# A transformer block on one core: heads normalised with VectorE's block transposes, and moved to the contraction's rows by small transfers

## The chip, the cores and the metric

The kernel runs on one core of a Trainium2 chip. The metric is the device time of one execution in microseconds (us). Five engines work beside each other, each through its own instructions in order: TensorE (PE in the profile, its weight loads PEld), VectorE (DVE), ScalarE (ACT), GpSimd (POOL) and SyncE (SP), which issues nearly all transfers (DMA). Matrix products land in PSUM, where the program has tiles of 512 fp32 a row: two times two of tag s, two of f, one each of m and a. Everything else lies in SBUF.

## The reference

Pre-norm attention with 32 query heads of width 18 over one shared key and value head, then a gated feed-forward without a nonlinearity. S = 2048, D = 576, F = 4608, all in fp32:

```python
def _A_ref(x, wq, wk, wv, wo):
    q = (x @ wq).reshape(B, S, H, Dh).transpose(0, 2, 1, 3)
    k = x @ wk
    v = x @ wv
    scores = jnp.einsum("bhqd,bkd->bhqk", q, k) * (Dh ** -0.5)
    p = _softmax(scores, axis=-1)
    o = jnp.einsum("bhqk,bkd->bhqd", p, v)
    return o.transpose(0, 2, 1, 3).reshape(B, S, H * Dh) @ wo
...
def _B_ref(x, w_gate, w_up, w_down):
    h = (x @ w_gate) * (x @ w_up)
    return h @ w_down
...
h = x + _A_ref(_layernorm(x), A_wq, A_wk, A_wv, A_wo)
h2 = h + _B_ref(_layernorm(h), B_w_gate, B_w_up, B_w_down)
```

## The kernel before

**Tiling.** The 2048 rows are worked in four blocks of 512 (b = 0 to 3), the 32 heads in eight groups of four (g = 0 to 7). For precision most products are made of a high and a low part of each operand (split, L91 and L92: a cast to the high part, a subtraction for the low part).

**Attention.** For one group and 128 keys, two steps of `pair` compute the scores of two heads each (L506, into PSUM of tag s, two buffers) and their exponential on ACT (L507). `flush` multiplies with the values (L511): four heads stand below each other in acc, 32 rows a head, of which row 0 is the softmax's sum (V has a column of ones) and rows 1 to 18 are the head. After 16 key tiles acc (128 x 512: rows are 4 heads x 32, columns are queries) is copied to os by VectorE (L522).

**Normalising a group** (`normal_heads`). Four PE transposes bring os to pt, with queries on the rows (L549); VectorE takes the reciprocal of the sums (L556; in block 0 a maximum with 1e-30 first, L553 and L554), and four multiplications write the heads to ob, 72 columns a group (L558). Two groups fill a chunk of 128 of the 576 columns. `chunk` transposes it back on PE (to, L140, four transposes), and splits it to o_hl (to oT in block 0), where the 576 columns are on the rows that the output projection contracts over. Chunk 4 has the last 64 columns twice, since its high and low part share a tile.

**Projecting.** `project` multiplies a chunk with its part of wo (yo, L625) and adds to the residual h on VectorE (L626). The weights wo of a chunk are loaded (wor, L587) when the chunk is split, and split one round later (wos).

**Order.** The program's order is written out by hand, and each engine follows it. Block 0's attention runs beside the query projections; the attention of block b + 1 runs inside the feed-forward of block b (`ffn`): 36 steps f, each with 54 products for gate and up (L818), a `pair` every four of them, and, in every second step, a down projection (`down`, L778) whose adds alternate between VectorE (L781) and ACT with GpSimd (L785, L786). Two steps of this kind are a period of some 31 us. What a group leaves to be done stands in a list, aux, and `run_aux` takes one entry at a time, of those whose round has come: at the end of each step f, and from step 26 (WITHIN) on also in the middle of a step (j = 12), there without the projections. Down weights (wdo, L709), gate and up weights (wr, L695) and the queries of the next group (q, L430 and L436) are loaded by SP, in the program's order.

**PSUM.** pt and to take the single buffer of tag m, or, at the end of a step (`at_end`), one half of a buffer of tag s (`ps_x`).

**The end.** In the last block, the last down pair (L744) has products for four row tiles s and two column halves n; ys of the last row tiles are halves of a tile of tag s, and each is added to h (L768) before the next product starts.

Of the kernel before, what the change touches and what calls it, by code (L numbers as in the profile page):

```python
# [16 lines left out]
F32 = mybir.dt.float32  # L17
# [3 lines left out]
ALU = mybir.AluOpType  # L21
# [13 lines left out]
HD = D // 2  # L35
# [22 lines left out]
class Block:  # L58
# [19 lines left out]
    def ps_y(self, i, name):  # L78
        return self.ps_m(name) if i % 3 == 1 else self.ps_f(name)

    def ps_x(self, name):

        return self.ps_s(name)[:, 0] if self.at_end else self.ps_m(name)

    def ps_a(self, name):
        return self.ps.tile([P, TB], F32, tag="a", bufs=1, name=name)

# [44 lines left out]
    def ln_apply(self, src, dst, mean, rstd):  # L132

        self.dve.tensor_scalar(dst[:, 0:D], src, mean, rstd, ALU.subtract, ALU.mult)
        self.dve.tensor_copy(dst[:, D:], dst[:, 512:D])

    def transposed(self, src, to, c, psum):

        for s in range(NQ):
            self.pe.transpose(psum[:, s * P:(s + 1) * P], src[:, s, c * P:(c + 1) * P], self.ident)  # L140
        if c < 4:
            self.split(*to, psum)
        else:
            self.split_tail(*to, psum)


    def keys_values(self):
# [257 lines left out]
    def again(self, g):  # L405

        q = self.pp.tile([P, 2, TB], F32R, tag="P", name=f"qa{g}")
        self.load_q(q, 0, g)
        self.load_m(q, 0, g)
        acc = self.ps_a(f"acca{g}")  # L410
        for t in range(NT):
            Ps = []
            for pr in range(2):
                s_ = self.ps_s(f"sa{g}_{t}_{pr}")
                p_ = self.pp.tile([P, 2, TB], F32, tag="P", name=f"Pa{g}_{t}_{pr}")
                self.scores(s_, p_, q, t, pr)
                Ps.append(p_)
            self.values(acc, Ps, t)
            del Ps, p_, s_
        os_ = self.os.get(g)  # L420
        if os_ is None:
            os_ = self.pp.tile([P, TB], F32, tag="P", name=f"osa{g}")
        self.dve.tensor_copy(os_, acc)
        if g not in self.os:
            self.normal_heads(0, g, os_)

# [87 lines left out]
    def flush(self, n):  # L514

        for b, g, t, Ps in self.pend[:n]:
            if t == 0:
                self.acc = self.ps_a(f"acc{b}_{g}")
            self.values(self.acc, Ps, t)
            if t == NT - 1:  # L520
                os_ = self.os[g] = self.op.tile([P, TB], F32, tag="os", bufs=1, name=f"os{b}_{g}")
                self.dve.tensor_copy(os_, self.acc)  # L522
                self.aux.append((self.round + 1, lambda b=b, g=g, o=os_: self.normalise(b, g, o), None))
        del self.pend[:n]

# [9 lines left out]

    def normalise(self, b, g, os_):
        if g == 0:
            self.ob = self.op.tile([P, NQ, 640], F32, tag="ob", name=f"ob{b}")
        self.normal_heads(b, g, os_)
        del self.os[g]  # L540
        for c in (g // 2,) * (g % 2) + (4,) * (b == 0 and g == NG - 1):
            self.aux.append((self.round, lambda c=c: self.chunk(b, c), None))

    def normal_heads(self, b, g, os_):

        pe, dve, ob = self.pe, self.dve, self.ob
        pt = self.ps_x(f"pt{b}_{g}")
        for s in range(NQ):
            pe.transpose(pt[:, s * P:(s + 1) * P], os_[:, s * P:(s + 1) * P], self.ident)  # L549
        p4 = pt.rearrange("p (s j c) -> p s j c", s=NQ, j=4)  # L550
        rc = self.op.tile([P, NQ, 4], F32, tag="rc", bufs=2, name=f"rc{b}_{g}")
        if b == 0:
            dve.tensor_scalar(rc, p4[:, :, :, 0], 1e-30, None, ALU.max)  # L553
            dve.reciprocal(rc, rc)  # L554
        else:
            dve.reciprocal(rc, p4[:, :, :, 0])  # L556
        for s in range(NQ):
            dve.tensor_tensor(ob[:, s, 72 * g:72 * g + 72].rearrange("p (j c) -> p j c", c=DH),  # L558
                              p4[:, s, :, 1:1 + DH],
                              rc[:, s, :].unsqueeze(2).broadcast_to([P, 4, DH]), ALU.mult)  # L560
        if g == NG - 1:
            dve.tensor_copy(ob[:, :, D:], ob[:, :, 512:D])

    def chunk(self, b, c):

# [13 lines left out]
        return [self.o_hl[:, 0], self.o_hl[:, 1]] if c < 4 else [self.o_hl[:, 0]]  # L579

    def chunk_of(self, b, c):
        self.transposed(self.ob, self.heads_to(b, c), c, self.ps_f(f"to{b}_{c}") if b == 0 and c == 4 else self.ps_x(f"to{b}_{c}"))


    def load_wo(self, c):
# [146 lines left out]
    def down(self, b, pair):  # L732

        pe, dve, act, sp, pool = self.pe, self.dve, self.act, self.sp, self.nc.gpsimd
        h = self.h[b]
        W = [self.wdo.pop((b, pair, j), None) for j in range(7)]
        if pair == NC - 1:
            ys = {}

            def part(s, n, i):  # L740

                ms = [(self.A[:, k, 2 * i + s // 2], W[(1, 0, 2, 3)[2 * i + n]][:, l]) for k, l in ((0, 0), (0, 1), (1, 0))]
                for j, (m, k) in enumerate(ms):
                    pe.matmul(ys[s, n][:, :HD], m[:, s % 2 * P:(s % 2 + 1) * P], k, start=(i == j == 0), stop=(i == 1 and j == 2))  # L744

            if b == NB - 1:
                e = self.ps_s("ye")
                for k, y in enumerate((e[:, 0], e[:, 1], self.ps_f("ye2"), self.ps_f("ye3"), self.ps_m("ye4"), self.ps_a("ye5"))):
                    ys[k // 2, k % 2] = y
                    part(k // 2, k % 2, 0)  # L750
            for s in range(NQ):
                for n in range(2):
                    if (s, n) not in ys:
                        if b < NB - 1:
                            ys[s, n] = self.ps_y(2 * s + n, f"y{b}_{pair}_{s}_{n}")
                        else:
                            e = self.ps_s("ye6") if n == 0 else e
                            ys[s, n] = e[:, n]
                        part(s, n, 0)
                    part(s, n, 1)  # L760
                    hs, y = h[:, s, n * HD:(n + 1) * HD], ys.pop((s, n))[:, :HD]
                    if b < NB - 1 and n:
                        z = self.tmp[:, self.n_tmp % 5]
                        self.n_tmp += 1
                        act.copy(z, y)
                        pool.tensor_tensor(hs, hs, z, ALU.add)
                    else:
                        dve.tensor_tensor(hs, hs, y, ALU.add)  # L768
                    yield
                sp.dma_start(self.out[b * TB + s * P: b * TB + (s + 1) * P, :], h[:, s, :])  # L770
            return
# [26 lines left out]
    def ffn(self, b):  # L798
        pe, act, dve = self.pe, self.act, self.dve
        X, hid, todo = self.X, [], None  # L800
        for f in range(NF):
# [11 lines left out]
            for c in range(9):  # L813
                for wk, xk in ((0, 0), (0, 1), (1, 0)):
# [7 lines left out]
                        self.split_w(n_ + 1)  # L822
                    if j == 5 and k:
                        self.left_first(n_ - 1, hid[0])
                    if j == 12 and f >= WITHIN:
                        self.run_aux(within=True)
                    if j == 21 and b == f == 0:
                        self.flush(len(self.pend))
# [18 lines left out]
                drain(self.down(b, *todo))  # L847
                self.load_wd(self.n_wd + 7)
            if f < NF - 1:
                self.at_end = True  # L850
                self.run_aux()
                self.at_end = False
            todo = (f // 2,) if k else None
        if b + 1 < NB:
            both(self.spread(b + 1), self.down(b, *todo))
# [92 lines left out]
    def run(self):  # L948
# [8 lines left out]
        self.h, self.qt, self.normed, self.wr, self.ws, self.wdo, self.wo_r, self.wos = {}, {}, {}, {}, {}, {}, {}, {}  # L957
        self.n_pair, self.half, self.pend, self.aux, self.round = 0, [], [], [], 0
        self.tqs = []
        self.at_end = False  # L960
        self.p2, self.p_next, self.wo_from, self.due = None, -1, 10 ** 6, 0.0
        with ExitStack() as st:
            pool = lambda name, bufs, **k: st.enter_context(tc.tile_pool(name=name, bufs=bufs, **k))
# [83 lines left out]

ORDER = (0, 3, 4, 2, 5, 6, 1)
WD_BUFS = 10
WITHIN = 26  # L1050
# [109 lines left out]
```

## Time and profile before

| | |
|---|---|
| median of 3 runs | 2378.72 us (2378.16 to 2379.43) |
| the profiled execution | 2379.29 us |
| its span in the trace | 2377.5 us |
| granted TensorE clock, mean | 0.994 |
| PE busy | 2319.2 us, 98% |
| ACT busy | 1434.3 us, 60% |
| VectorE busy | 1150.8 us, 48% |
| GpSimd busy | 644.5 us, 27% |
| SP queue (hardware DMA) | 326.6 MB, 42.6% of 16 engines |

Times in the trace's rows are us from the span's start; a row of the timeline has start, length, engine, line, operation, tiles written and read, shapes, count, and in brackets the idle time of its engine before it with what ended that. A row of a group has the tiles, the shape, the count, busy time and mean length (ns), and idle time. SPq is SP's queue of issues. Names are the program's own, without buffer numbers.

### The profile page before, as it was taken

The numbers are of one execution on the slowest core, as the hardware profiler recorded it, in microseconds if no ns is written. First come the engines' busy times: TensorE is split into PE (matmuls) and PEld (weight loads), VectorE is DVE, ScalarE is ACT, GpSimd is POOL, SyncE is SP. The second block draws the span as 40 slices with busy tenths as digits, with TensorE's granted clock in tenths as the row PEclk, the third lists the DMA queues.
The fourth block names the chain that finished last, engine by engine and source line by source line (L and its number), as shares of the span: only waits on it lengthen the run. The fifth ranks groups of instructions, "written<-read, shape, count | busy, mean of one in ns | idle before, by whom it ended". The sixth has DMA issues, their size and how long they took to land.

```text
span 2377.5 us, 46287 instructions
## 1 busy us (share of the span) xinstructions
PE 2319.2 (98%) x18425; PEld 1630.6 (69%) x18425; DVE 1150.8 (48%) x2130; ACT 1434.3 (60%) x1869; POOL 644.5 (27%) x803
## 2 busy tenths in 40 slices
PE   5999989999999999999999999999999999999999
PEld 4333434677777777777776777767777788888888
DVE  7545534344443444544444445433444367565565
ACT  4787867766667665676666666566666622232322
POOL 3535400122212222222222122212222233343333
PEclk9999999999999999999999999999999999999999
DMA  4677860433333333533333333453333344655553
GB/s 139 207 256 249 282 214 19 139 123 107 114 99 117 118 123 113 170 123 118 119 105 116 103 123 118 135 157 118 122 114 110 95 156 161 200 191 184 174 166 125
DMA packets 154086, 340.23 MB, mean 143 GB/s; under 512 B 14760, under 2 KB 47016, under 8 KB 153864
## 3 DMA queue, kind: packets, MB, share of 16 engines
q1 hardware_dynamic: 151272, 326.59, 42.6%
q0 software_dynamic: 2592, 10.62, 1.6%
q8 instruction: 147, 2.41, 0.4%
q14 instruction: 75, 0.61, 0.1%
HBM read 272.63 MB, written 55.67 MB: 138 GB/s over the span
## 4 chain that ended last, share of the span: by engine, by line
PE 82%; DVE 1%; ACT 1%; DMA 1%; issue 0%; SPq 0%; ACTq 0%; DVEq 0%
PE y L778 17%; PE pg L818 16%; PE acc L511 15%; PE gu L818 12%; PE s L506 9%; PE pu L818 9%; PE yo L625 3%; PE y L744 1%; PE pt L549 1%; ACT P L507 1%; PE tx L674 0%; PE to L140 0%; PE ye L744 0%; DMA X<-X 0%; DMA out_dram<-h 0%
## 5 line engine op out<-in xcount | busy, mean ns | idle before, releaser
L507 ACT ACTIVATE P<-s 128x1024 f32<-128x1024 f32 x1024 | 1027.3, 1026 | 337.3 <-PE s L506 259.4
L818 PE MATMUL pu<-X,ws 64*128 64x512 f32 x2565 | 701.3, 391 | 0.0
L818 PE MATMUL pg<-X,ws 64*128 64x512 f32 x2565 | 701.3, 391 | 0.0
L786 POOL TENSOR_TENSOR h<-h,tmp 128x288 f32<-128x288 f32 x408 | 318.5, 811 | 938.3 <-ACT tmp L785 937.0
L818 PEld LDWEIGHTS pg<-X,ws 64*128 64x128 f32 x2565 | 475.8, 186 | 57.3 <-issue 1.5
L511 PE MATMUL acc<-P,V 128*32 128x512 f32 x4096 | 492.4, 600 | 4.8 <-DVE os L522 4.0
L818 PEld LDWEIGHTS pu<-X,ws 64*128 64x128 f32 x2565 | 473.7, 186 | 30.2
L506 PE MATMUL s<-q,kT 56*128 56x512 f32 x2048 | 442.1, 425 | 10.0 <-SPq L396 6.4
L778 PEld LDWEIGHTS y<-wdo,room 128*128 128x128 f32 x2856 | 386.0, 188 | 48.7 <-issue 45.8
L778 PE MATMUL y<-wdo,room 128*128 128x288 f32 x2856 | 403.4, 300 | 1.3 <-DVE h L781 1.2
L785 ACT COPY tmp<-y 128x288 f32<-128x288 f32 x408 | 162.7, 399 | 326.6 <-PE y L778 321.4
L781 DVE TENSOR_TENSOR h<-h,y 128x288 f32<-128x288 f32 x544 | 235.3, 454 | 243.6 <-PE y L778 241.1
L506 PEld LDWEIGHTS s<-q,kT 56*128 56x128 f32 x2048 | 196.9, 185 | 204.8 <-ACT P L507 109.8
L818 PE MATMUL gu<-X,ws 64*128 64x512 f32 x2646 | 308.8, 389 | 2.0 <-DVE hf L840 1.7
L818 PEld LDWEIGHTS gu<-X,ws 64*128 64x128 f32 x2646 | 256.0, 184 | 47.9 <-issue 4.1
L511 PEld LDWEIGHTS acc<-P,V 128*32 128x32 f32 x4096 | 114.6, 109 | 253.1 <-issue 232.0
L91 POOL CAST ws<-wr 128x1152 fp32r<-128x1152 f32 x144 | 165.7, 1151 | 436.8 <-PE pu L818 177.4
L840 DVE TENSOR_TENSOR hf<-pu,g 128x512 f32<-128x512 f32 x95 | 65.7, 692 | 380.1 <-ACT g L836 376.8
L92 DVE TENSOR_TENSOR ws<-wr,ws 128x1152 fp32r<-128x1152 f32 x144 | 194.9, 1354 | 60.4 <-POOL ws L91 60.4
L92 DVE TENSOR_TENSOR room<-S,room 128x1024 fp32r<-128x1024 f32 x68 | 83.3, 1225 | 143.7 <-ACT room L91 143.7
L836 ACT COPY g<-gu 128x512 f32<-128x512 f32 x49 | 28.9, 590 | 133.5 <-PE gu L818 133.5
L91 ACT CAST room<-hf 128x256 fp32r<-128x256 f32 (+1 forms) x144 | 73.9, 513 | 45.0 <-DVE hf L840 44.7
(169 smaller groups left out, 1594.3 us busy)
## 6 DMA issues: line engine op xcount, KB each, us to landing
wdo<-wd_dram SPq DMA_DIRECT2D x492, 288.0 KB
wr<-in_wgu_dram SPq DMA_DIRECT2D x144, 576.0 KB
wd_dram<-wd_room SPq DMA_DIRECT2D x20, 1008.0 KB
q<-q_dram SPq DMA_DIRECT2D x64, 216.0 KB
q_dram<-qs SPq DMA_DIRECT2D x16, 504.0 KB
X<-X SPq DMA_DIRECT2D x28, 256.0 KB
wd_dram<-wd_hi SPq DMA_DIRECT2D x7, 1008.0 KB
wd_dram<-wd_src SPq DMA_DIRECT2D x7, 1008.0 KB
```

The costliest lines, as they stand in the source:

```text
L91: (copy or self.cast)(hi, src)
L92: self.dve.tensor_tensor(lo, src, f32(hi), ALU.subtract)
L506: self.pe.matmul(s_[:, i], self.kT[o:o + 56, t * P:(t + 1) * P], q[o:o + 56, pr], start=True, stop=True)
L507: self.act.activation(p_, s_, AF.Exp, scale=SCALE)
L511: self.pe.matmul(acc[32 * j:32 * j + 32, :], self.V[:, t, :], Ps[j // 2][:, j % 2, :], start=(t == 0), stop=(t == NT - 1), skip_group_chec ...
L625: pe.matmul(y[:, :HD], m, k, start=(i == 0), stop=(i == len(ms) - 1))
L778: pe.matmul(y[:, :HD], m[:, t * P:(t + 1) * P], k, start=(first and j == 0), stop=(j == 2), skip_group_check=True)
L781: dve.tensor_tensor(hs, hs, y[:, :HD], ALU.add)
L785: act.copy(z, y[:, :HD])
L786: pool.tensor_tensor(hs, hs, z, ALU.add)
L818: pe.matmul(ps, w[o:o + 64, wk, c], X[o:o + 64, xk, c], start=(j == 0), stop=(j == 26))
L840: dve.tensor_tensor(hf, pu, g, ALU.mult)
```

## The change

os is made by a transpose of VectorE in blocks of 32 x 32 straight from acc, in place of the copy. Then each row of os is a query modulo 32, and its 512 columns are 16 pieces of 32, a piece for each run of 32 queries, with the sum in column 0 and the head in columns 1 to 18. One reciprocal and one multiplication normalise all of it in place, and a second block transpose brings the heads back below each other, into a free part of ob. From there 18 rows of 512 at a time are moved by SP to the rows that the contraction wants: a head is one transfer, or two where it crosses a chunk's end, and twice as many in chunk 4; 40 a block. A chunk is then split from ob as it stands. No PE transpose is left in either step. With them go `ps_x`, `at_end` and `transposed`. `run_aux` is called in the middle of every step f, and in block 0 a chunk is due two rounds later. In the last pair of the last block both halves are multiplied before either is added.

```diff
@@ flush, again
-                self.dve.tensor_copy(os_, self.acc)
+                self.dve.transpose(os_, self.acc)
@@ normalise
-            self.ob = self.op.tile([P, NQ, 640], F32, tag="ob", name=f"ob{b}")
+            self.ob = self.op.tile([P, 5, TB], F32, tag="ob", name=f"ob{b}")
...
-            self.aux.append((self.round, lambda c=c: self.chunk(b, c), None))
+            self.aux.append((self.round + (2 if b == 0 else 0), lambda c=c: self.chunk(b, c), None))
@@ normal_heads
-        pt = self.ps_x(f"pt{b}_{g}")
-        for s in range(NQ):
-            pe.transpose(pt[:, s * P:(s + 1) * P], os_[:, s * P:(s + 1) * P], self.ident)
-        p4 = pt.rearrange("p (s j c) -> p s j c", s=NQ, j=4)
-        rc = self.op.tile([P, NQ, 4], F32, tag="rc", bufs=2, name=f"rc{b}_{g}")
+        o = os_.rearrange("p (k c) -> p k c", c=32)
+        rc = self.op.tile([P, TB // 32], F32, tag="rc", bufs=2, name=f"rc{b}_{g}")
         if b == 0:
-            dve.tensor_scalar(rc, p4[:, :, :, 0], 1e-30, None, ALU.max)
+            dve.tensor_scalar(rc, o[:, :, 0], 1e-30, None, ALU.max)
             dve.reciprocal(rc, rc)
         else:
-            dve.reciprocal(rc, p4[:, :, :, 0])
-        for s in range(NQ):
-            dve.tensor_tensor(ob[:, s, 72 * g:72 * g + 72].rearrange("p (j c) -> p j c", c=DH),
-                              p4[:, s, :, 1:1 + DH],
-                              rc[:, s, :].unsqueeze(2).broadcast_to([P, 4, DH]), ALU.mult)
-        if g == NG - 1:
-            dve.tensor_copy(ob[:, :, D:], ob[:, :, 512:D])
+            dve.reciprocal(rc, o[:, :, 0])
+        dve.tensor_tensor(o[:, :, 1:1 + DH], o[:, :, 1:1 + DH],
+                          rc.unsqueeze(2).broadcast_to([P, TB // 32, DH]), ALU.mult)
+        turned = ob[:, 4 if g < NG - 1 else 0]
+        dve.transpose(turned, os_)
+        for j in range(4):
+            r, end = DH * (4 * g + j), DH * (4 * g + j + 1)
+            p = 32 * j + 1
+            while r < end:
+                c, n = r // P, min(end, (r // P + 1) * P) - r
+                for q in (r % P, 64 + r % P)[:1 if c < 4 else 2]:
+                    self.sp.dma_start(ob[q:q + n, c], turned[p:p + n])
+                r, p = r + n, p + n
@@ chunk_of
-        self.transposed(self.ob, self.heads_to(b, c), c, self.ps_f(f"to{b}_{c}") if b == 0 and c == 4 else self.ps_x(f"to{b}_{c}"))
+        (self.split if c < 4 else self.split_tail)(*self.heads_to(b, c), self.ob[:, c])
@@ down, the last pair
                     part(s, n, 1)
-                    hs, y = h[:, s, n * HD:(n + 1) * HD], ys.pop((s, n))[:, :HD]
-                    if b < NB - 1 and n:
...
-                        dve.tensor_tensor(hs, hs, y, ALU.add)
+                    if b < NB - 1:
+                        add(s, n)
+                        yield
+                if b == NB - 1:
+                    for n in range(2):
+                        add(s, n)
                     yield
@@ ffn
-                    if j == 12 and f >= WITHIN:
+                    if j == 12:
                         self.run_aux(within=True)
...
-                self.at_end = True
                 self.run_aux()
-                self.at_end = False
```

What this moves is shown at one place of the program on three engines: block 1, groups 1 and 2, inside the feed-forward of block 0. On PE, this stood at the end of a step without a down projection (acc are the value products of group 2, s its scores, pg and pu gate and up):

```order
L511 MATMUL acc_2_11537<-P_2_3_0_11512,V 32x512 x2
L511 MATMUL acc_2_11537<-P_2_3_1_11525,V 32x512 x2
L549 MATMUL pt_1_11554<-C,os_1_11338 128x128 x4
L506 MATMUL s_2_4_0_11567<-q_2_10816,kT 128x512 x2
L818 MATMUL pg_11565<-X_10540,ws_11434 128x512
```

and now:

```order
L498 MATMUL acc_2_11471<-P_2_3_0_11446,V 32x512 x2
L498 MATMUL acc_2_11471<-P_2_3_1_11459,V 32x512 x2
L493 MATMUL s_2_4_0_11494<-q_2_10753,kT 128x512 x2
L817 MATMUL pg_11492<-X_10468,ws_11359 128x512
L817 MATMUL pu_11493<-X_10468,ws_11359 128x512
```

The four transposes are gone, and the scores follow the value products. On VectorE, over the same step (ws and room are split weights and hidden values, hf gate times up, S sums of hf for the down projection), before:

```order
L92 TENSOR_TENSOR ws_11434<-wr_11104,ws_11434 128x1152
L92 TENSOR_TENSOR room<-hf_11320,room 128x256
L840 TENSOR_TENSOR hf_11529<-pu_11420,g_11522 128x512
...
L92 TENSOR_TENSOR room<-hf_11529,room 128x512
L556 RECIPROCAL rc_1_11559<-pt_1_11554 128x16
L558 TENSOR_TENSOR ob_10872<-pt_1_11554,rc_1_11559 128x72 x4
L92 TENSOR_TENSOR ws_11580<-wr_11233,ws_11580 128x1152
```

and now:

```order
L88 TENSOR_TENSOR ws_11359<-wr_11029,ws_11359 128x1152
L88 TENSOR_TENSOR room<-hf_11245,room 128x256
L541 RECIPROCAL rc_1_11399<-os_1_11263 128x16
L542 TENSOR_TENSOR os_1_11263<-os_1_11263,rc_1_11399 128x16x18
L545 STREAM_TRANSPOSE ob_10720<-os_1_11263 128x512
L839 TENSOR_TENSOR hf_11463<-pu_11345,g_11456 128x512
...
L88 TENSOR_TENSOR room<-hf_11463,room 128x512
L88 TENSOR_TENSOR room<-ob_10720,room 128x512
L88 TENSOR_TENSOR ws_11507<-wr_11158,ws_11507 128x1152
```

The normalisation has moved from the step's end to its middle, ahead of hf, and the split of chunk 0 (room<-ob) has come to the step's end, from the end of the next step. On SP, between the load of wr in this step and that in the next, before:

```order
L695 DMA wr_11437<-in_wgu_dram 128x1152
L430 DMA q_3_11498<-q_dram 54x2x512 x2
L436 DMA q_3_11498<-m_dram 2x2x512 x2
L695 DMA wr_11583<-in_wgu_dram 128x1152
L709 DMA wdo_3_2_11753<-wd_dram 128x576
```

and now:

```order
L686 DMA wr_11362<-in_wgu_dram 128x1152
L552 DMA ob_10720<-ob_10720 18x512 x3
L552 DMA ob_10720<-ob_10720 2x512
L552 DMA ob_10720<-ob_10720 16x512
L417 DMA q_3_11432<-q_dram 54x2x512 x2
L423 DMA q_3_11432<-m_dram 2x2x512 x2
L578 DMA wor_11490<-in_wo_dram 128x576
L686 DMA wr_11510<-in_wgu_dram 128x1152
```

The five transfers of group 1 stand ahead of the next group's queries, and the load of wor, which stood behind seven loads of wdo a step later, has come ahead of them and of the next wr.

More of the change, by code (lines that the diff above doesn't have):

```diff
@@ L79, in ps_y @@
         return self.ps_m(name) if i % 3 == 1 else self.ps_f(name)
-    def ps_x(self, name):
-        return self.ps_s(name)[:, 0] if self.at_end else self.ps_m(name)
     def ps_a(self, name):
@@ L135, in ln_apply @@
         self.dve.tensor_copy(dst[:, D:], dst[:, 512:D])
-    def transposed(self, src, to, c, psum):
-        for s in range(NQ):
[L140 to L144, printed above, removed]
     def keys_values(self):
@@ L422, in again @@
             os_ = self.pp.tile([P, TB], F32, tag="P", name=f"osa{g}")
-        self.dve.tensor_copy(os_, acc)
+        self.dve.transpose(os_, acc)
         if g not in self.os:
@@ L541, in normalise @@
         for c in (g // 2,) * (g % 2) + (4,) * (b == 0 and g == NG - 1):
-            self.aux.append((self.round, lambda c=c: self.chunk(b, c), None))
+            self.aux.append((self.round + (2 if b == 0 else 0), lambda c=c: self.chunk(b, c), None))
     def normal_heads(self, b, g, os_):
-        pe, dve, ob = self.pe, self.dve, self.ob
-        pt = self.ps_x(f"pt{b}_{g}")
-        for s in range(NQ):
-            pe.transpose(pt[:, s * P:(s + 1) * P], os_[:, s * P:(s + 1) * P], self.ident)
-        p4 = pt.rearrange("p (s j c) -> p s j c", s=NQ, j=4)
-        rc = self.op.tile([P, NQ, 4], F32, tag="rc", bufs=2, name=f"rc{b}_{g}")
+        dve, ob = self.dve, self.ob
+        o = os_.rearrange("p (k c) -> p k c", c=32)
+        rc = self.op.tile([P, TB // 32], F32, tag="rc", bufs=2, name=f"rc{b}_{g}")
         if b == 0:
-            dve.tensor_scalar(rc, p4[:, :, :, 0], 1e-30, None, ALU.max)
+            dve.tensor_scalar(rc, o[:, :, 0], 1e-30, None, ALU.max)
             dve.reciprocal(rc, rc)
         else:
-            dve.reciprocal(rc, p4[:, :, :, 0])
-        for s in range(NQ):
-            dve.tensor_tensor(ob[:, s, 72 * g:72 * g + 72].rearrange("p (j c) -> p j c", c=DH),
-                              p4[:, s, :, 1:1 + DH],
-                              rc[:, s, :].unsqueeze(2).broadcast_to([P, 4, DH]), ALU.mult)
-        if g == NG - 1:
-            dve.tensor_copy(ob[:, :, D:], ob[:, :, 512:D])
+            dve.reciprocal(rc, o[:, :, 0])
[11 more added lines that the diff above has]
+                r, p = r + n, p + n
     def chunk(self, b, c):
@@ L750, in down, with add @@
                     part(k // 2, k % 2, 0)
+            def add(s, n):
+                hs, y = h[:, s, n * HD:(n + 1) * HD], ys.pop((s, n))[:, :HD]
+                if b < NB - 1 and n:
+                    z = self.tmp[:, self.n_tmp % 5]
+                    self.n_tmp += 1
+                    act.copy(z, y)
+                    pool.tensor_tensor(hs, hs, z, ALU.add)
+                else:
+                    dve.tensor_tensor(hs, hs, y, ALU.add)
             for s in range(NQ):
@@ L760, in down @@
                     part(s, n, 1)
-                    hs, y = h[:, s, n * HD:(n + 1) * HD], ys.pop((s, n))[:, :HD]
-                    if b < NB - 1 and n:
[L763 to L768, printed above, removed]
+                    if b < NB - 1:
[4 more added lines that the diff above has]
+                        add(s, n)
                     yield
@@ L959, in run @@
         self.tqs = []
-        self.at_end = False
         self.p2, self.p_next, self.wo_from, self.due = None, -1, 10 ** 6, 0.0
@@ L1049 @@
 WD_BUFS = 10
-WITHIN = 26
 WO_FROM = 208
```

## The prediction

> **What bounds the kernel.** I read the page first: the share of each engine and the chain that ended last.
>
> ```profile
> span 2377.5 us, 46287 instructions
> PE 2319.2 (98%) x18425; PEld 1630.6 (69%) x18425; DVE 1150.8 (48%) x2130; ACT 1434.3 (60%) x1869; POOL 644.5 (27%) x803
> PE 82%; DVE 1%; ACT 1%; DMA 1%; issue 0%; SPq 0%; ACTq 0%; DVEq 0%
> ```
>
> TensorE (PE) is busy 98% of the span and is 82% of the chain; no other engine passes 60%. A busy PE can hide slack, because ends of matmuls are modelled, and a share is a mean over stages. So I next cut the execution into stages with the view of stretches (columns: length, then busy time of PE, weight loads, VectorE, ScalarE, GpSimd; granted clock, DMA share, GB/s).
>
> ```profile
> 60.00:330.00 270.00, 261.89 (x1906) 106.07 (x1908) 142.08 (x204) 214.78 (x221) 114.11 (x128) 0.98 0.74 239
> 330.00:420.00 90.00, 79.35 (x508) 35.70 (x500) 36.20 (x95) 60.42 (x65) 7.05 (x11) 0.94 0.30 99
> 420.00:960.00 540.00, 538.16 (x4392) 381.21 (x4394) 231.59 (x448) 366.30 (x468) 116.51 (x135) 1.00 0.37 115
> 960.00:1500.00 540.00, 539.04 (x4416) 387.29 (x4410) 240.00 (x455) 359.51 (x466) 126.63 (x150) 1.00 0.39 123
> 1500.00:1905.00 405.00, 403.34 (x3308) 289.44 (x3306) 171.05 (x314) 267.76 (x346) 92.14 (x109) 1.00 0.40 124
> ```
>
> From 420 to 1905 us, where 23 of the 32 head groups are normalised, PE has 4.5 us free in 1485 and ScalarE (ACT) has about 491 us free. PE is the limit there, at full clock, and what leaves PE leaves the time, unless a new wait takes its place. From 60 to 330 PE has 97%; from 330 to 420, where attention runs without the feed-forward beside it, 88%, and there a saving may be lost.
>
> **What is removed from PE.** Two groups of transposes (last numbers: busy us, mean ns, idle before).
>
> ```profile
> L549 PE MATMUL pt<-C,os 128*128 128x128 f32 x128 | 21.1, 288 | 0.4 <-DVE os L522 0.4
> L140 PE MATMUL to<-C,ob 128*128 128x128 f32 x80 | 12.6, 280 | 2.4 <-DVE ob L558 2.4
> 507.35 0.66 PE L549 MATMUL pt<-C,os 128*128 128x128 f32 x4
> 507.93 0.50 PE L506 MATMUL s<-q,kT 56*128 56x512 f32 x2
> 525.97 0.60 PE L140 MATMUL to<-C,ob 128*128 128x128 f32 x4
> 526.50 0.50 PE L506 MATMUL s<-q,kT 56*128 56x512 f32 x2
> ```
>
> There are 208 transposes in 52 groups of four, 33.7 us busy. As they overlap their neighbours, I take the time from the first transpose's start to the start of what follows: 0.58 us (507.35 to 507.93) and 0.53 (525.97 to 526.50). With 0.57 for each, 52 groups are **29.6 us**. Busy time gives 33.7 as the upper end, 0.53 a group 27.6 as the lower.
>
> Waits of PE that stand at these transposes go with them:
>
> ```profile
> 225.25 0.63 PE L140 MATMUL to<-C,ob 128*128 128x128 f32 x4 [2.43 <-DVE ob L558]
> 1908.64 6.44 PE L818 MATMUL gu<-X,ws 64*128 64x512 f32 x54 [0.91 <-DVE hf L840]
> 1922.16 1.21 PE L818 MATMUL gu<-X,ws 64*128 64x512 f32 x8 [0.80 <-DVE hf L840]
> ```
>
> At 225 us PE waits 2.43 us for the normalised heads. At 1908 and 1922 the transposes had taken one of the two buffers of tag s, and the next gate product waits for the other. Sum **4.1 us**.
>
> **The last pair of the last block** gets its two adds behind both products, so PE no longer waits for an add before it writes the other half of the same tile:
>
> ```profile
> 2369.12 3.04 PE L744 MATMUL ye<-wdo,room 128*128 128x288 f32 x21 [0.55 <-DVE h L768]
> 2372.71 1.06 PE L744 MATMUL ye<-wdo,room 128*128 128x288 f32 x6 [0.55 <-DVE h L768]
> 2373.80 0.46 DVE L768 TENSOR_TENSOR h<-h,ye 128x288 f32<-128x288 f32 x1 [1.15 <-PE ye L744]
> ```
>
> 1.1 us of idle goes; at the end two adds follow the last product instead of one, 0.4 more. Net **0.7 us**.
>
> **What VectorE does instead.** Before, a group costs a copy of 0.69, a reciprocal of 0.26 and four multiplications that take 0.65 together (508.33, below). After, it costs a block transpose out of PSUM, a reciprocal, one multiplication of 288 elements (0.46 in the add of 288 just shown) and a block transpose in SBUF. No row here shows a block transpose. The nearest row is the copy of the same 128x512:
>
> ```profile
> L522 DVE COPY os<-acc 128x512 f32<-128x512 f32 x32 | 22.1, 691 | 55.0 <-PE acc L511 54.0
> 550.67 2.56 PE L778 MATMUL y<-wdo,room 128*128 128x288 f32 x17
> 550.81 0.69 DVE L522 COPY os<-acc 128x512 f32<-128x512 f32 x1 [2.23 <-PE acc L511]
> 551.42 0.81 DVE L781 TENSOR_TENSOR h<-h,y 128x288 f32<-128x288 f32 x2
> ```
>
> I take 0.69 for each, as an estimate, so VectorE gains about 0.5 us a group, covered by idle time (642.6 us busy of 1485 from 420 to 1905). The bounds are 0.42 (a 256-element pass, below) and twice 0.69. Above 0.69 it has a price: in blocks 1 and 3 the copy stands directly ahead of the adds that empty PE's banks (550.81, then 551.42), and PE takes up a bank again as soon as it is added. So each 0.1 us above 0.69 costs up to 0.1 us in some 15 groups: nothing as chosen, 10 us at the upper end. The Trainium skill's "VectorE: DVE Perf Modes", section "The three transpose paths", has 311 ns for 128x128 in bf16 and "32×32 blocks only"; with 384 more columns at one per cycle of 0.96 GHz that is an estimate of 711 ns, and no run here shows it.
>
> The casts and subtractions that split a chunk now read SBUF, where they read PSUM: for 128x512 0.61 against 0.59 us on ACT (505.85, below), nothing.
>
> **What moves.** Normalisation comes half a feed-forward step earlier (middle instead of end), the split of chunk c takes the place of the last normalisation, and the output projection moves up likewise; that is the same PE work at places of the same kind. What is new is that the split waits for transfers: 40 a block, 160 in all, of 36 KB (18 rows of 2 KB), issued by SP behind the block transpose. For group 1 of block 1 the rows of today are:
>
> ```profile
> 498.79 0.42 DVE L92 TENSOR_TENSOR room<-hf,room 128x256 fp32r<-128x256 f32 x1
> 504.48 0.69 DVE L840 TENSOR_TENSOR hf<-pu,g 128x512 f32<-128x512 f32 x1 [5.26 <-ACT g L836]
> 508.33 0.65 DVE L558 TENSOR_TENSOR ob<-pt,rc 128x72 f32<-128x72 f32 x4
> 498.90 0.33 SPq L695 DMA_DIRECT2D wr<-in_wgu_dram  x1
> 505.85 0.61 ACT L91 CAST room<-hf 128x512 fp32r<-128x512 f32 x1
> 508.53 1.03 ACT L507 ACTIVATE P<-s 128x1024 f32<-128x1024 f32 x1 [2.07 <-PE s L506]
> ```
>
> VectorE is free from 499.21 for 5.26 us: reciprocal, multiplication and transpose end at about 500.6. SP issues five transfers at 0.33 each until 502.3. They must land before ACT's new cast, which stands behind the cast of 505.85 (end 506.46); ACT then has nothing to do until 508.53, and the new cast takes 0.61. So a landing up to 5.6 us after the last issue (502.3 to 507.9) costs nothing. How long is a landing?
>
> ```profile
> 521.29 5.18 SPq L709 DMA_DIRECT2D wdo<-wd_dram  x7
> 526.53 0.42 SPq L587 DMA_DIRECT2D wor<-in_wo_dram  x1
> 532.02 0.67 POOL L91 CAST wos<-wor 128x576 fp32r<-128x576 f32 x1 [3.95 <-DMA wor<-in_wo_dram]
> POOL wos L91 <- DMA wor<-in_wo_dram: 47.4, 10, 8.6
> ```
>
> The 288 KB of wor, issued right behind seven loads of 288 KB, are there after 5.5 us (526.53 to 532.02). The new 36 KB stand behind one load of 576 KB (498.90) alone, so less: I count **0**. In block 2 the split comes a whole down-projection later, with more room. The loads queued behind the transfers on SP (the next group's q, wor, wr) are due one group or half a step later; SP itself waits 1452 us in these two rows alone:
>
> ```profile
> SPq L695 <- DVE ws L92: 758.2, 89, 26.5
> SPq L709 <- PE y L778: 693.7, 441, 13.3
> ```
>
> Between 386 and 400 us, the end of block 0, there is a cost. Chunk 4 needs nine transfers (9 x 0.33 = 3.0 us) and its cast comes two rounds later in ACT's queue, where ACT is the slower engine. The cast of chunk 4 stands today 4.4 us behind the exponential of 386.51, beside which the heads are transposed:
>
> ```profile
> 386.51 1.02 ACT L507 ACTIVATE P<-s 128x1024 f32<-128x1024 f32 x1 [0.25 <-PE s L506]
> 390.95 0.59 ACT L100 CAST oT<-to 128x512 fp32r<-128x512 f32 x1
> ```
>
> After, 1.4 of VectorE and 3.0 of issue are these 4.4 already, a landing comes on top, and two more exponentials (1.02 each) cover 2.0 of it. With a landing of 3.5 I charge **1.5 us** (0 to 4 for landings of 2 to 6).
>
> A rule of the Trainium skill speaks against all this. "DMA: Bandwidth & Descriptors", section "Rules for kernel authors", says to coalesce small transfers, since below 64 KB one pays mostly overhead, and its section on the anatomy of one DMA puts the fixed part at about 2 us. Were the fixed parts paid one after the other, five transfers would be an estimated 10 us, 4.4 beyond the 5.6. Seven loads issued within 5.18 us and an eighth, all landed by 532.02, show that they overlap.
>
> **Sum.** The profiled execution took 2379.3 us (span 2377.5 and 1.8 around it), 0.6 above the median of the runs. 2379.3 - 29.6 - 4.1 - 0.7 + 1.5 = 2346.4; against the median 2345.8. I say **2346 us**, 1.4% faster.
>
> **Rivals.** (1) *A block transpose takes twice the copy.* Then 15 groups lose 0.69 each, 10 us: 2356. For it: no row shows the operation. Against it: the passes over 512 elements quoted here, a copy and a product, take 0.69 alike.
>
> (2) *The transfers land late and ACT stands still, slower than before.* ACT works in order, so while the cast waits, no exponential runs, and PE, with two score buffers, stops soon after. Price: landing minus 5.6 us, in the 15 chunks of blocks 1 to 3. It equals the gain of 33 at a landing of 7.8 us; at 9 us it is 51, giving 2346 + 51 = 2397. For it: GpSimd waited up to 8.6 us for wor, and between 60 and 330 us DMA is busy at 74%. Against it: the wor of 5.5 us stood behind 2 MB of loads, and from 420 on DMA is busy at 37 to 40%. By the skill's rule the price would be 15 x 4.4 = 66, or 2412.
>
> (3) *Half the gain goes into VectorE's order.* VectorE stands ahead of every bank that PE wants back. If the 0.5 us more of each group is passed on to PE, 32 groups lose 16 us: 2362. For it: PE takes banks up at once. Against it: the idle 5.26 us at the very place.
>
> (4) *The change does not shorten the chain*: PE's busy time is modelled, and ACT bounds the attention, so that the transposes filled holes: 2377. Against it: ACT has a third of its time free from 420 to 1905.
>
> **Chances.** Forecast (2340 to 2352) 0.62; rival 1 0.10; rival 3 0.10; rival 2 0.10, of which 0.02 stays below the old time; rival 4 0.05; the rest 0.03 is a gain above the forecast. The range is 2339 to 2364: upwards it takes in rivals 1 and 3, downwards the 33.7 us of busy time with 4.1 and 1.1 (2340). Within 0.2% (4.8 us, about what a measurement here can tell from no change) lies rival 4, 0.05; slower 0.08; faster the other 0.87.
>
> **What would show it.** Right: no matmul out of os or ob; PE busy near 2286 us at 98% again; block transposes at 0.7 us; ACT's idle time ahead of the casts from ob without a wait on their DMA above some 2 us; no wait ahead of the ye products. Wrong: "ACT room" or "DVE oT" waiting for the DMA of ob by tens of us in sum (rival 2), block transposes above 1 us with PE y waiting for DVE h (rival 1), PE pg or y waiting for DVE (rival 3).

## The result, and the profile after

The changed kernel takes **2362.3 us** (median of 8 runs, 2357.7 to 2368.8) against 2379.0 (8 runs, 2376.9 to 2382.0): a ratio of 0.993, 95% interval 0.9916 to 0.9945. It is faster by 16.7 us; 33 were forecast. The time lies in the range, above the forecast's 2340 to 2352; the sign is right, and half of the gain is missing.

The page after: span, engines, and the chain that ended last by engine.

```profile
span 2359.8 us, 46074 instructions
PE 2291.4 (97%) x18217; PEld 1604.3 (68%) x18217; DVE 1165.5 (49%) x2062; ACT 1433.4 (61%) x1869; POOL 647.8 (27%) x803
PE 80%; DVE 2%; issue 1%; ACT 1%; DMA 1%; POOL 1%; SPq 0%; DVEq 0%; ACTq 0%; POOLq 0%
```

The 208 transposes are gone (18425 matmuls before, 18217 now), and PE's busy time fell by 27.8 us. But the span fell only by 17.7: PE is idle for 10 us more. The view of waits, PE's alone (who waited for whom: total us, times, longest), says behind whom; waits that are as long in the kernel before are left out here:

```profile
PE psq L329 <- DVE qs L336: 7.5, 3, 6.2
PE yo L616 <- DVE h L617: 6.3, 5, 5.2
PE y L777 <- DVE h L780: 5.1, 2, 3.9
```

Three single waits of 6.2, 5.2 and 3.9 us, all on VectorE. Where they stand in time shows when the same matmul is looked up in both traces. The two kernels share all other matmuls, so the start before minus the start after is the lead that the changed kernel has won by then. The table gives the lead won in each stretch (bounded by the last value product of block 0, the first of block 1's second group, the last one of all, and a gate product 100 us later), beside the forecast's terms for the same stretch. The columns to the right are experiments that follow below; each column is one profiled execution.

| stretch, time of before (us) | forecast | changed | no_transfers | twice | wor_first | gpsimd_half | late_split | late_split_no_wd_load |
|---|---|---|---|---|---|---|---|---|
| 0 to 385.4 | 8.1 | -0.2 | 2.1 | -8.7 | 3.8 | 0.9 | 2.0 | 10.3 |
| 385.4 to 443.7 | 0.2 | -5.1 | 1.8 | -12.5 | -5.3 | -1.7 | -5.2 | -5.6 |
| 443.7 to 1894.3 | 20.5 | 24.0 | 24.1 | -6.1 | 23.4 | 24.5 | 23.2 | 22.6 |
| 1894.3 to 1994.9 | 3.4 | -2.4 | 3.4 | -8.5 | 0.8 | 2.3 | -1.6 | -1.5 |
| 1994.9 to the end | 0.7 | 1.4 | 1.3 | 1.4 | 1.4 | 1.3 | 1.3 | 1.3 |
| span | 32.9 | 17.7 | 32.7 | -34.4 | 24.1 | 27.3 | 19.7 | 27.1 |

(The forecast's 29.6 for 52 groups is spread here as 10, 3, 36 and 3 groups of 0.57; its 2.43, 1.7, 0.7 and -1.5 stand where it put them.) In the long middle the change does all that was expected and 3.5 us more. It loses 8 us against the forecast before 385, 5 at the end of block 0 and 6 at the end of block 3. The three places, from the timeline, the two ends first:

**The end of block 0** (start, length, engine, line, operation, tiles; idle before and what ended it).

```profile
387.95 0.71 DVE L545 STREAM_TRANSPOSE ob<-os 128x512 f32<-128x512 f32 x1
388.69 6.71 SPq L552 DMA_DIRECT2D ob<-ob  x9
397.06 0.62 ACT L96 CAST oT<-ob 128x512 fp32r<-128x512 f32 x1 [4.53 <-DMA q<-m_dram]
397.71 0.69 DVE L97 TENSOR_TENSOR oT<-ob,oT 64x512 fp32r<-64x512 f32 x1 [5.38 <-ACT oT L96]
398.94 1.09 PE L616 MATMUL yo<-wo,oT 128*128 128x288 f32 x3 [5.23 <-DVE h L617]
```

SP needs 6.71 us to issue the nine transfers that I had put at 3.0. The last issue ends at 395.40, its rows are there 1.7 us later, and only then ScalarE casts chunk 4; VectorE's subtraction and the adds to h stand behind the cast, PE behind the adds. Behind this wait PE runs at half its clock from 398.94 to 403.05 (granted clock 0.50), which costs 2.1 us more. (The row names a load of q as what ended ScalarE's wait; the cast reads ob alone, and the issue just ahead is ob's.)

**The end of block 3**, where the group's nine transfers and the weight chunk wor follow each other on SP:

```profile
1887.21 7.04 SPq L552 DMA_DIRECT2D ob<-ob  x9
1894.30 0.47 SPq L578 DMA_DIRECT2D wor<-in_wo_dram  x1
1897.37 0.67 POOL L87 CAST wos<-wor 128x576 fp32r<-128x576 f32 x1 [7.73 <-DMA wor<-in_wo_dram]
1898.07 1.33 DVE L88 TENSOR_TENSOR wos<-wor,wos 128x576 fp32r<-128x576 f32 x1 [3.10 <-POOL wos L87]
1899.32 0.81 DVE L780 TENSOR_TENSOR h<-h,y 128x288 f32<-128x288 f32 x2
1899.82 6.94 PE L777 MATMUL y<-wdo,room 128*128 128x288 f32 x33 [3.90 <-DVE h L780]
```

Read it backwards: PE waits for an add, the add stands behind VectorE's split of wor, that behind GpSimd's cast, that behind wor's load, and the load behind nine transfers that it has nothing to do with.

**The stage up to 330 us**, at 225:

```profile
224.39 0.71 DVE L545 STREAM_TRANSPOSE ob<-os 128x512 f32<-128x512 f32 x1
225.34 7.61 SPq L552 DMA_DIRECT2D ob<-ob  x5
233.52 0.50 DVE L87 CAST oT<-ob 128x512 fp32r<-128x512 f32 x1 [8.42 <-DMA ob<-ob]
235.14 3.61 DVE L926 TENSOR_TENSOR wd_src<-wd_src,wd_hi 128x864 f32<-128x864 f32 x2
238.67 0.68 DVE L336 COPY qs<-psr 126x512 f32<-126x512 f32 x1
239.41 0.70 PE L329 MATMUL psq<-XT,wq_h 64*72 64x512 f32 x1 [6.21 <-DVE qs L336]
```

In block 0 the split's cast is VectorE's own, and it stands directly behind the block transpose: two rounds later in the program are no distance in VectorE's queue when no other work of its own lies between. VectorE stands still for 8.4 us, and the copy of q that PE waits for stands behind it.

Here the issue is the smaller part. The five transfers are those of group 3, whose heads fill rows 216 to 288: only the first three carry rows of chunk 1 (128 to 255), for which the cast waits. The third of them is this row:

```profile
227.83 0.63 SPq L552 DMA_DIRECT2D ob<-ob  x1
```

It ends at 228.46, and the cast starts 5.1 us later, where it was 1.7 us at the end of block 0. So what is late here is the landing. Why it is longer here is not shown.

All three places stand behind these transfers. The changed kernel's transfers by line (times are shortest, median and longest, in ns), and under it on-chip transfers that stood in the trace of before:

```profile
L552 SPq DMA_DIRECT2D ob<-ob x160: 560/703/1602, 105.6 to 1893.6; - x160
```

```profile
L686 SPq DMA_DIRECT2D X<-X x36: 462/588/1194, 416.7 to 2040.2; - x36
```

An issue costs SP 0.70 us (the median), not 0.33. I had taken 0.33 from a load out of DRAM; the trace of before had transfers of the same kind, on-chip memory to on-chip memory, at 0.59.

### The profile page after: what moved, and what is told of

The parts are those of the page before. It is cut to its first block, busy times and chain, and to the rows that moved or that the text cites. A ratio compares the mean times of both kernels' runs of the same rounds, so it can differ in the third digit from the quotient of the medians.

```text
span 2359.8 us, 46074 instructions
## 1 busy us (share of the span) xinstructions
PE 2291.4 (97%) x18217; PEld 1604.3 (68%) x18217; DVE 1165.5 (49%) x2062; ACT 1433.4 (61%) x1869; POOL 647.8 (27%) x803
## 4 chain that ended last, share of the span: by engine, by line
PE 80%; DVE 2%; issue 1%; ACT 1%; DMA 1%; POOL 1%; SPq 0%; DVEq 0%; ACTq 0%; POOLq 0%
PE y L777 16%; PE pg L817 15%; PE acc L498 15%; PE gu L817 12%; PE pu L817 9%; PE s L493 9%; PE yo L616 2%; PE y L735 1%; ACT P L494 0%; POOL h L785 0%; PE ye L735 0%; PE tx L665 0%; SPq L552 0%; DMA out_dram<-h 0%; DMA X<-X 0%
```

## The experiments

**Theory T**: the missing gain is lost at these three places, where an engine that works in order stands behind the small transfers. **Rival V** is the third one of the prediction (half the gain goes into VectorE's order), whose number, 2362, is the measured one.

### again and no_transfers

The changed kernel unaltered, and the changed kernel with the block transpose writing the split's rows itself:

```diff
-        turned = ob[:, 4 if g < NG - 1 else 0]
-        dve.transpose(turned, os_)
-        for j in range(4):
...
-                    self.sp.dma_start(ob[q:q + n, c], turned[p:p + n])
+        dve.transpose(ob[:, g // 2 if g % 2 else 4], os_)
```

> The changed kernel once more, for the spread of its runs and for a second trace. Theory T (the gain that is missing, about 16 us, is lost at three places where an engine that works in order stands behind the small transfers: 9.7 us at 225 to 255 us, 5 to 7 us at 390 to 402 us, about 4 us at 1896 to 1900 us): all three waits come back within 1 us each, time about 2362. Rival V (half the gain goes into VectorE's order, 0.5 us in each of 32 groups): no fixed places, time about 2362 too. If the first wait is an accident of the load on the DMA engines, it comes out shorter here, down to nothing, and the time falls towards 2353.

> Leaves the 160 transfers out: the block transpose writes the split's rows directly, so the heads stand in wrong rows; every instruction of TensorE, VectorE, ScalarE and GpSimd stays. Theory T: the three waits go (9.7 + 6 + 4 us), 2343 to 2347 us. Rival V: the work of VectorE is the same, so the time stays at 2360 to 2364.

Measured: again 2362.9 us (0.9937, 0.9924 to 0.9951), no_transfers **2347.0** (0.9864, 0.9849 to 0.9879). In again two of the three waits come back as they were (5.2 and 3.9 us), but the first is 2.7 us and not 6.2, where theory T expected it within 1 us. All of VectorE's work is still in no_transfers, so rival V is out: the number fitted, the mechanism didn't. The ends of block 0 and of block 3 come back as forecast (1.8 and 3.4 in the table), and their waits are gone from the list. But the first stage does not come back: 2.1 of 8.1, with no transfer in it. PE's longest waits there from 60 to 330 us, and what VectorE and GpSimd were doing:

```profile
PE psq L329 <- DVE qs L336: 4.5, 1, 4.5
PE acc L498 <- DVE os L509: 3.2, 3, 2.0
```

```profile
284.62 3.18 POOL L903 TENSOR_TENSOR wd_room<-wd_room 128x288 f32<-128x288 f32 x4 [6.16 <-DMA wd_room<-in_wd_dram]
288.69 1.96 DVE L917 TENSOR_TENSOR wd_room<-wd_room 128x864 f32<-128x864 f32 x1 [8.57 <-POOL wd_room L911]
291.31 0.63 PE L329 MATMUL psq<-XT,wq_h 64*126 64x512 f32 x1 [4.49 <-DVE qs L336]
```

A load of down weights comes late for GpSimd, GpSimd for VectorE's subtraction, and the copy of q stands behind that: the same kind of wait, with the transfers gone. In the trace of again the first stage won 4.1 us, in that of the changed kernel it lost 0.2, and the program is the same: this stage moves by some 4 us from one execution to the next. So theory T holds for two places; at the third the transfers were late too, but without them the stage is hardly better, and a new theory is needed (W, below).

### twice

Each transfer as two of half the rows; bytes as before.

```diff
-                    self.sp.dma_start(ob[q:q + n, c], turned[p:p + n])
+                    m = n // 2
+                    self.sp.dma_start(ob[q:q + m, c], turned[p:p + m])
+                    self.sp.dma_start(ob[q + m:q + n, c], turned[p + m:p + n])
```

> Each transfer is issued as two of half the rows: the same bytes, 320 issues on SP instead of 160. Theory T (the price is the issue, 0.70 us of SP each whatever the rows, one behind the other): the last cast of block 0 waits for nine more issues, 6.3 us; the load of wor at the end of block 3 comes 6.3 us later as well: 2373 to 2377 us, and more where chunk 4 of blocks 1 and 2 loses its cover too (up to 2389). Rival B (the price is in the bytes or in the landing): 2360 to 2365.

Measured: **2413.7 us** (1.0145, 1.0124 to 1.0165), slower than before the change, by more than either number expected. The first of the two halves, and PE's waits:

```profile
L553 SPq DMA_DIRECT2D ob<-ob x160: 551/698/1447, 107.2 to 1944.9; - x160
```

```profile
PE yo L618 <- DVE h L619: 18.1, 7, 11.0
PE y L779 <- DVE h L782: 11.4, 2, 10.2
PE psq L329 <- DVE qs L336: 9.3, 2, 5.4
```

Half the rows cost the same 0.70: the price is the issue, not the bytes (rival B is out). The end of block 0 loses 7.4 us more than the changed kernel and the end of block 3 6.1 (the table), where nine more issues are 6.3. Beyond that the middle, untouched by 160 issues, loses 30 us to 320: its cover is used up somewhere between. By the same lookup of matmuls, 5.0 and 10.0 us of it are lost around chunk 4 of blocks 1 and 2, and 3.0 to 3.8 behind each of four other chunks of blocks 2 and 3. Which engine ended these waits was not followed further.

### wor_first

```diff
+        if b and g % 2:
+            self.load_wo(g // 2)
         self.normal_heads(b, g, os_)
...
-        else:
+        elif c == 4:
             self.load_wo(c)
```

> The load of the output weight's chunk is issued ahead of the heads' transfers of the same chunk instead of behind them. Theory T: at the end of block 3 GpSimd's cast of wor no longer comes late, VectorE's subtraction and the adds behind it neither, PE's wait of 3.9 us ahead of y at 1896 us goes: 2357 to 2359 us. If the adds there are late for VectorE's own work (rival V), the time stays at 2362.

Measured: **2356.1 us** (0.9908, 0.9893 to 0.9923), 6.8 less than again. At the end of block 3:

```profile
1882.63 0.43 SPq L580 DMA_DIRECT2D wor<-in_wo_dram  x1
1883.99 7.16 SPq L554 DMA_DIRECT2D ob<-ob  x9
1888.29 1.01 POOL L87 CAST wos<-wor 128x576 fp32r<-128x576 f32 x1 [7.46 <-DMA wor<-in_wo_dram]
1894.28 6.21 PE L779 MATMUL y<-wdo,room 128*128 128x288 f32 x33 [1.24 <-DVE h L782]
```

The nine issues still take 7.16 us, but GpSimd has wor before they end and PE waits 1.24 us instead of 3.90. In the table that is 3.2 us (from -2.4 to 0.8). The traced execution is 6.4 us shorter than that of the changed kernel, but 4.0 of this lie in the first stage, which moves by itself (again has 4.1 there as well), and I don't count them for the edit.

### gpsimd_half, wor_and_gpsimd, wor_and_gpsimd_all

The four transfers that fill the upper half of chunk 4 leave from GpSimd's queue:

```diff
-                for q in (r % P, 64 + r % P)[:1 if c < 4 else 2]:
-                    self.sp.dma_start(ob[q:q + n, c], turned[p:p + n])
+                self.sp.dma_start(ob[r % P:r % P + n, c], turned[p:p + n])
+                if c == 4:
+                    q = 64 + r % P
+                    self.nc.gpsimd.dma_start(ob[q:q + n, c], turned[p:p + n])
```

> The four transfers of each block that fill the upper half of chunk 4 are issued by GpSimd instead of SP. Theory T: five issues of 0.70 in a row instead of nine; the cast of chunk 4 in block 0 finds its rows 2.8 us earlier and the wor of block 3 leaves 2.8 us earlier: 2357 to 2359 us. If a transfer that GpSimd issues lands later than SP's nine do, the cast at 397 us does not move and only the end of block 3 gains: 2359 to 2361.

> The load of wor ahead of the heads' transfers (as in the run that did this alone, 2356), and in block 0 alone the upper half of chunk 4 issued by GpSimd. Theory T: the two places add, 2.8 us less than 2356: 2352 to 2354. If GpSimd's transfers land late: 2356.

> wor first, and the upper half of chunk 4 issued by GpSimd in all blocks (no late split). Theory T: the end of block 0 as in the run with GpSimd (3.4 us gained), and the ends of the blocks no better than with either alone, since both take away the same wait for wor: 2352 to 2355. If the issue on SP were still what is late there, the two would add: 2349 to 2351.

Measured: gpsimd_half **2353.7 us** (0.9897, 0.9882 to 0.9912), better than expected; wor_and_gpsimd (GpSimd in block 0 only) 2355.5 (0.9903, 0.9888 to 0.9918); wor_and_gpsimd_all **2352.9** (0.9882, 0.9867 to 0.9897). In gpsimd_half, at the end of block 0:

```profile
387.60 3.74 SPq L551 DMA_DIRECT2D ob<-ob  x5
387.87 2.05 POOL L554 DMA_DIRECT2D ob<-ob  x4 [50.38 <-DVE ob L545]
392.89 0.62 ACT L96 CAST oT<-ob 128x512 fp32r<-128x512 f32 x1 [1.04 <-DMA ob<-ob]
```

From SP's first issue to the cast are 5.3 us (387.60 to 392.89) where there were 8.4 (388.69 to 397.06): 3.1 less, as 4 x 0.74 says, and the table has 3.4. The end of block 3 gains 4.7 by the same five issues. Putting wor first as well adds nothing that shows: both edits take away the same wait. From 385.4 us on wor_and_gpsimd wins 26.7 us and gpsimd_half 26.4; in the first stage, which these edits don't touch, the one trace lost 2.7 and the other won 0.9, and that is the difference of their times.

### late_split, late_split_late_wd, late_split_no_wd_load

**Theory W**: the stage up to 330 us has a second bound, the down weights that are prepared beside the attention (load, sums and cast by GpSimd, subtraction by VectorE), so that a wait removed there comes back at the next place. First the split behind the next copy of q, then also the first of the two subtractions one round later, then, instead, 14 of the 18 loads left out:

```diff
-            self.aux.append((self.round + (2 if b == 0 else 0), lambda c=c: self.chunk(b, c), None))
+            self.aux.append((self.round + ((5 if c < 3 else 2) if b == 0 else 0), lambda c=c: self.chunk(b, c), None))
```

```diff
-                         (2, lambda p=p: high(p)), (4, lambda p=p: low(p, 0)), (5, lambda p=p: low(p, 1))):
+                         (2, lambda p=p: high(p)), (5, lambda p=p: low(p, 0)), (5, lambda p=p: low(p, 1))):
```

```diff
-            pool.dma_start(where[p][0][:, 0:4], self.wd[p])
+            if p in (0, 1, 5, 10):
+                pool.dma_start(where[p][0][:, 0:4], self.wd[p])
```

> In block 0 the split of chunks 0 to 2 is put three rounds later, behind the next group's q on VectorE; transfers and their issue stay. Theory T: PE's wait of 6.2 us at 233 to 239 us and the slow matmuls after it go, 2352 to 2355 us; the other two places stay. If the DMA engines' load is what is late (and not the cast ahead of the q copies), the wait turns up again at the later cast: 2359 to 2363. Rival V: 2362.

> The late split of block 0 (2359.6 alone), and the first of VectorE's two subtractions on each group of prepared down weights one round later, behind the next copy of q instead of ahead of it. Theory W (the stage from 60 to 330 us is also held by the down weights: load, cast by GpSimd, subtraction by VectorE, and only then the copy for which PE waits; so a wait removed at 233 us came back at 290 us): now neither stands, the stage gains 4 to 6 us more, 2354 to 2356. If the wait at 290 us has another cause, it stays: 2358 to 2361.

> The late split of block 0 once more (2359.6 alone), with 14 of the 18 loads of down weights left out in the stage up to 330 us: the prepared weights of those groups are stale, every cast, subtraction and store on them stays. Theory W in its wider form (the loads of the down weights, each 7 to 9 us until GpSimd may cast, set VectorE's order in that stage, and moving one subtraction only moved the wait): PE's wait of 4.7 us at 292 us goes and comes up nowhere else in the stage, so PE stands 6 to 8 us ahead of the kernel before at 375 us instead of 2.0, and the time is 2353 to 2356. If VectorE's own work or GpSimd's casts hold the stage, the wait stays: 2358 to 2361.

Measured: late_split 2359.6 us (0.9915, 0.9901 to 0.9928), late_split_late_wd 2361.4 (0.9919, 0.9905 to 0.9932), late_split_no_wd_load **2353.4** (0.9896, 0.9880 to 0.9913). The first line of PE's waits from 60 to 330 us, in this order of kernels:

```profile
PE psq L329 <- DVE qs L336: 4.7, 1, 4.7
```

```profile
PE acc L498 <- DVE os L509: 7.1, 3, 4.5
```

```profile
PE acc L498 <- DVE os L509: 3.7, 3, 2.6
```

With the split moved, the wait at 233 us is gone and PE is 6.1 us ahead at 270; at 292 it waits 4.7 us behind the subtraction of down weights, and the lead at 385 is 2.0; the forecast of 2352 to 2355 was missed. With that subtraction behind the copy of q as well, what stands behind it now is the block transpose that frees the value products' bank, and PE waits 4.5 us there, at 295 to 300. This edit was expected to gain 4 to 6 us and gained nothing: theory W as I first had it, a matter of which row stands behind which, fell. With the loads left out, no wait above 2.6 us is left, PE stands 10.3 us ahead at 385 (8.1 forecast), and the time is 6.2 below late_split. This is one trace, but the eleven others (without twice) have between -2.7 and 4.1 at 385. So the pace of the loads holds this stage, and the order on VectorE only chooses where PE pays. Leaving out loads also takes bytes from the DMA engines (share 0.67 instead of 0.76 from 60 to 330 us); whether the loads are late by their own length or by the traffic beside them, these runs don't tell apart.

### all_three and all_four

Late split, wor first and GpSimd's half in one, and the later subtraction on top.

> Late split in block 0, wor first, and the upper half of chunk 4 issued by GpSimd in all blocks. If the three places were independent: 2356 - 3 - 3 = 2350. If the late split's gain at 250 us only runs into the next wait at 290 us (as its own trace shows: 8.7 gained, 5.8 lost again), and GpSimd's issues cost its own casts something in blocks 1 to 3: 2353 to 2357.

> All edits together: late split and late down weights in block 0, wor first, the upper half of chunk 4 issued by GpSimd. Theories T and W: the run with three of them (2354) less the 4 to 6 us of the stage from 60 to 330 us, 2348 to 2351. If PE's wait in that stage only finds a third place, 2353 to 2356.

Measured: 2354.0 us (0.9900, 0.9885 to 0.9915) and 2352.6 (0.9886, 0.9871 to 0.9901). Neither differs from wor_and_gpsimd_all by more than the intervals; the two edits of block 0 are worth nothing here, as late_split_late_wd said. The version to keep is gpsimd_half or wor_and_gpsimd_all: 25 to 27 us less than before and about 9 less than the changed kernel, with a handful of lines.

## Why the prediction was right, and where it was not

**Transposes out of PE (29.6).** Right, and too small: in the 36 groups between 443.7 and 1894.3 the lead grows by 24.0 us, 0.67 a group and not 0.57 if all of it is put down to them; the busy time, 33.7 / 52 = 0.65, was the better row than the distance of two starts. PE's busy time, forecast as 2286 us at 98%, is 2291 at 97%, and 2287 at 98% without transfers.

**Waits that go with them (4.1).** The 0.91 and 0.80 at gate products went (gate products wait 0.3 us in all now, 2.0 before). The 2.43 at 225 us went as well and another wait came to the same stage; on the split of block 0's chunks 0 to 2, whose cast is VectorE's and waits for the transfers, the prediction has no term (VectorE stood still for 16.9 us in three such waits). The step that failed is the one before it: "From 60 to 330 PE has 97%" was read as PE's bound with 3% of slack. It is a stage with two bounds close together, and what a stage is worth can't exceed the distance to the second. The prediction's fourth rival, that the chain isn't shortened, comes out for this stage alone (8.1 forecast, -0.2 and 4.1 won in two executions), but not for the reason that it gave, a bound by ScalarE.

**The last pair (0.7).** Right in kind, half the size: 1.4 measured from 1994.9 us to the end. PE's two waits of 0.55 us are gone; where the rest comes from was not followed.

**Block transposes (0.69 each).** Right, and rival 1 is out:

```profile
L509 DVE STREAM_TRANSPOSE os<-acc 128x512 f32<-128x512 f32 x32 | 22.9, 716 | 55.0 <-PE acc L498 54.0
L545 DVE STREAM_TRANSPOSE ob<-os 128x512 f32<-128x512 f32 x32 | 22.8, 712 | 1.1
```

The Trainium skill's "VectorE: DVE Perf Modes", section "The three transpose paths", gave an estimate of 711 ns by adding columns to its 128x128; 712 are measured out of SBUF and 716 out of PSUM, so the trace agrees.

**Transfers land in time (0).** Right for every group of blocks 1 to 3 but the last of block 3: with 160 transfers and with none the middle wins 24.0 and 24.1. Wrong in two steps. The issue: "five transfers at 0.33 each" are 0.70 each, hidden in the middle and not at the ends. And the queue: "the loads queued behind the transfers on SP (the next group's q, wor, wr) are due one group or half a step later" doesn't hold for the last group, whose chunk, and with it wor's load, follows at once; 5.8 us lost against the forecast (3.4 to -2.4), 5.8 back without transfers.

**The end of block 0 (+1.5).** The place was named and the mechanism was right: transposes, nine issues, a landing, two exponentials as cover. The term was mis-sized, in both directions: the nine issues took 6.7 instead of 3.0, the landing 1.7 instead of 3.5, and with these two the prediction's own sum gives 3.4. Measured against no_transfers it is 6.9 (1.8 to -5.1). PE's wait accounts for 4.9 of it (5.2 against 0.3) and the half clock behind the wait, for which the sum had no term, for about the other 2; why the wait is 4.9 and not 3.4 stays open.

**Rivals.** Of rival 2 (an engine stands still behind a late transfer) the mechanism is there, but in block 0 and not in the 15 chunks of blocks 1 to 3. At the end of block 0 it was mostly the issues that were late, at 225 us the landing. Rivals 1 and 3 are out, by the rows above and by no_transfers. The range reached up to 2364 only to take in these two, and neither came about: that 2362 lies in it is luck. The sum without transfers, 32.7, is the forecast's 32.9 almost to the tenth, but partly by luck: the first stage is 6 us short and the middle 3.6 over.

## What to carry to other kernels

Price a transfer twice: what its issue takes from the queue that sends it, times the number in a row, and its landing once behind the last (1.7 us at one place here, 5.1 at another). Take the price from a row of the same kind of memory at both ends, and look at the burst, not at the mean: 0.37 us too little each cost nothing that shows in the 23 groups of the middle; the two ends, where nine stood ahead of something due, lost 11 us. Before crediting a stage with a saving, ask what its second bound is; a wait that only changes its place when the order is altered points to a producer behind it.

## What the runs showed of the hardware

**An issue's price hardly depends on the rows.** SP takes 0.70 us (medians) for 18 rows of 2 KB and for 9 rows, 0.59 for X's 256 KB; GpSimd took 0.51 for the same rows (2.05 for four). The landing, 1.5 to 1.7 us behind the last issue's end (395.40 to 397.06 in the changed kernel, 391.34 to 392.89 in gpsimd_half), was paid once. At 228 us it was 5.1. The Trainium skill's "DMA: Bandwidth & Descriptors", section "Anatomy of one DMA — SWDGE (gpsimd) path", has about 2 us fixed for each transfer that GpSimd issues. Here, on SP, issue and landing make some 2.4 us at the end of block 0 (0.70 and 1.7), of which the 0.70 are paid one after the other and the rest overlaps.

**A stall of PE costs more than its idle time.** Stretches of the changed kernel: ahead of the wait at 233 us, the wait itself, behind it, and once more; then behind the wait at the end of block 0 (the number ahead of the DMA share is the granted clock).

```profile
222.00:232.00 10.00, 10.00 (x80) 4.18 (x80) 3.00 (x5) 8.38 (x9) 1.47 (x2) 1.00 0.61 192
232.00:239.40 7.40, 1.20 (x10) 0.19 (x2) 5.82 (x6) 2.14 (x3) 7.25 (x6) 0.76 0.73 247
239.40:246.00 6.60, 6.57 (x26) 2.21 (x30) 4.63 (x6) 2.39 (x3) 0.93 (x2) 0.50 1.03 332
246.00:254.00 8.00, 8.00 (x64) 2.85 (x58) 0.00 (x0) 6.56 (x7) 2.61 (x4) 1.00 1.02 345
398.94:403.05 4.11, 4.11 (x15) 3.18 (x16) 1.68 (x5) 1.94 (x2) 0.00 (x0) 0.50 0.04 11
```

After 6.2 us of idle PE runs at half its clock for 6.6 us: 3.3 us more, so that this wait cost 9.5. None of the prediction's prices for a wait had that. The Trainium skill's "TensorE: Matmul & The Clock Gate", section "Part 1: The HAM clock gate (the "warmup" mystery)", has the clock at half after an idle window of about 3.4 us; the trace agrees for this stall, with a longer tail here than one such window of busy time. A shorter stall did it too: behind the 2.43 us of idle at 225 us in the kernel before, the granted clock was 0.64 over 3.6 us, 1.3 us more.

```profile
225.20:228.80 3.60, 3.55 (x20) 1.78 (x22) 2.85 (x4) 0.59 (x1) 3.06 (x3) 0.64 0.74 172
```
